# Fused attention, soft mixture of experts and feed-forward: the opening's loads issued together, q on a second queue, and ScalarE's opening order written out

## The chip, the cores and the metric

The kernel runs on one core of one Trainium2 chip. Its time is the device time of one execution in microseconds (us). The engines are named as in the profile: PE (TensorE; PEld is its weight load), DVE (VectorE), ACT (ScalarE), POOL (GpSimd), and SP (SyncE), whose queue issues transfers.

## What is computed

Three layers in one launch, all in float32, with B, H, S, D = 8, 8, 576, 64:

```python
# 1: attention, block causal (blocks of 64 positions)
scores = q @ k.T / sqrt(D); masked where block(query) < block(key)
x = softmax(scores) @ v            # x: 4608 tokens by 512
# 2: soft mixture of experts, 8 experts of 4 slots
logits = x @ phi                   # phi: 512 by 32
slot_input = softmax over tokens(logits).T @ x
slot_out = relu(slot_input[e] @ w1[e]) @ w2[e]
x = softmax over slots(logits) @ slot_out
# 3: feed-forward
h = relu(x @ w_in);  out = (h * h) @ w_out
```

## The kernel before

Attention is worked in 32 pairs of heads, n = 0 to 31: pair n is heads j and j+4 of batch b, with b, j = divmod(n, 4). For a pair, `load_pair(n)` (line 292) issues four transfers of 128 KB, two halves of k and two of q (L298); for the first pair of a batch four more of 64 KB (L305) bring the last 64 positions of k and q of the whole batch. Even batches land in the tile `ar_lo`, odd ones in `ar_hi`; v goes to `ar_hi`. All of these are issued on SP's queue, in SP's order of instructions.

What then happens to a pair, with the names that the profile shows:

- `scale` (line 318): ACT squares k and q and sums them (`square`, L324, tile `junk`); PE adds the sums over partitions (`chain`, L331, `ps_ssq`); eight small DVE operations (L334 to L353) make from them two scales, `sig`, for k and q.
- `split` (line 364): ACT rounds k and q times the scale to float16 (`high`, L383, tiles `ka` and `qa`), DVE makes the rest (`low`, L387); a transfer turns k (`prep_k`, L394, `s<-ka`), and PE turns q (`turn_q`, L403, `ps_qT`), from where ACT copies it out (L407, tile `t`).
- `maxpass` (line 411): PE makes scores for the row maxima (L419, L427, L454, `ps_max`), DVE reduces them (L433), puts the result in extra columns of the low part of q, and a transfer turns this (L480, `t<-qb`). `s2copy` (L895, `s<-s`) copies the turned low part of k beside constants.
- `scores` (L496, L505, L514, `ps_sc`) with the exponentials on ACT (L534, L516), then `pv` (L569 to L606) with v.

The function `pair(n)` (line 925) interleaves these for neighbouring pairs: `scores(n)`, `maxpass(n + 2)`, `split(n + 3)`, `pv(n - 1)`. Loads wait in a list, `dq`; `loads(k)` issues up to k from its front. In the opening (lines 888 to 920) pairs 0 to 2 are prepared ahead of the loop. PE's order inside the loop is the order of the code (`manual_schedule`); the order of the other engines, and of SP's transfers, is chosen by the tile scheduler from the dependences and the order of the code.

```python
loads(12)
prepare()
order = lambda p: [p[2], p[0], p[3], p[1]]   # prep_k, high_q, low_q, turn_q
...
loads(LR if n else 1)                        # in pair(n), eight times; LR = 4
```

The scheduler gives each transfer one of eight semaphores in turn; a transfer waits until the one eight before it has landed.

Of the kernel before, what the change touches and what calls it, by code (L numbers as in the profile page):

```python
# [23 lines left out]
def tile_attn_soft_moe_ffn(  # L24
# [12 lines left out]
    nc = tc.nc  # L37
# [168 lines left out]
    def attention():  # L206
# [82 lines left out]
                in_=phi.rearrange("(hp j p) s -> hp p j s", hp=2, p=64)[hp],  # L289
            )  # L290

        def load_pair(n):
            b, j = divmod(n, NJ)
            t = qk_tile(b)

            def main(nm, hp):
                src = dict(q=q, k=k)[nm][b]
                nc.sync.dma_start(  # L298
                    out=t[nm][:, hp:2 * NU:2, j, :],
                    in_=src[NJ * hp + j, 0:128 * NU, :].rearrange("(u p) d -> p u d", p=128),  # L300
                )

            def tail(nm, hp):
                src = dict(q=q, k=k)[nm][b]
                nc.sync.dma_start(  # L305
                    out=t[nm][64 * hp:64 * hp + 64, 2 * NU],
                    in_=src[NJ * hp:NJ * hp + NJ, 128 * NU:S, :].rearrange("j i d -> i j d"),
                )

            fs = []  # L310
            for nm in "kq":
                for f in (tail, main) if j == 0 else (main,):
                    fs += [lambda f=f, nm=nm, hp=hp: f(nm, hp) for hp in range(2)]
            return fs
# [3 lines left out]
        def scale(ns):  # L318
            w = len(ns)
            small = lambda nm, k=2, bufs=2: sm_p.tile([128, k, 2], F32, tag=nm, name=nm, bufs=bufs)[:, :, 0:w]  # L320
            ssq = sm_p.tile([128, 2, w], F32, tag=f"ssq{w}", name="ssq")

            def square(i, nm, c):
                nc.scalar.activation(  # L324
                    out=junk, in_=qk_tile(ns[c] // NJ)[nm][:, :, ns[c] % NJ, :], func=AF.Square, accum_out=ssq[:, i, c:c + 1],
                    saturate=False,
                )

            def chain():
                ps = ps_r.tile([128, 512], F32, tag="r", name="ps_ssq")  # L330
                nc.tensor.matmul(ps[:, 0:2 * w], ones[:, 0:1].to_broadcast([128, 128]), ssq.rearrange("p a c -> p (a c)"), start=True, stop=True)  # L331
                a, hb, g, inv = [small(nm) for nm in ("sc_a", "sc_h", "sc_g", "inv")]
                sig, es = small("sig", bufs=4), small("es", 1, 4)
                nc.vector.tensor_scalar(  # L334
                    out=a, in0=ps[:, 0:2 * w].rearrange("p (a c) -> p a c", a=2), scalar1=1e-30, scalar2=None, op0=ALU.max
                )
                nc.vector.tensor_scalar(
                    out=hb.bitcast(U32), in0=a.bitcast(U32), scalar1=1, scalar2=0x7F800000,
                    op0=ALU.logical_shift_right, op1=ALU.bitwise_and,
                )  # L340
                nc.vector.tensor_scalar(
                    out=g.bitcast(U32), in0=hb.bitcast(U32), scalar1=0x7F800000, scalar2=None,
                    op0=ALU.bitwise_xor,
                )
                nc.vector.tensor_scalar(out=sig, in0=g, scalar1=2.0 ** -51, scalar2=None, op0=ALU.mult)
                nc.vector.tensor_scalar(out=inv, in0=hb, scalar1=2.0 ** 50, scalar2=None, op0=ALU.mult)
                nc.vector.scalar_tensor_tensor(
                    out=sig[:, 1], in0=inv[:, 0], scalar=2.0 ** 20, in1=sig[:, 1], op0=ALU.mult, op1=ALU.min
                )
                nc.vector.scalar_tensor_tensor(  # L350
                    out=inv[:, 1], in0=sig[:, 0], scalar=2.0 ** -20, in1=inv[:, 1], op0=ALU.mult, op1=ALU.max
                )
                nc.vector.scalar_tensor_tensor(  # L353
                    out=es[:, 0], in0=inv[:, 0], scalar=1.0 / float(D) ** 0.5, in1=inv[:, 1],
                    op0=ALU.mult, op1=ALU.mult,
                )
                for c, n in enumerate(ns):
                    sc[n] = (sig[:, :, c], es[:, 0, c:c + 1])

            return [lambda i=i, nm=nm, c=c: square(i, nm, c) for c in range(w) for i, nm in ((1, "k"), (0, "q"))] + [chain]  # L360
# [3 lines left out]
        def split(n):  # L364
            b, j = divmod(n, NJ)
            if n in (1, 3):
                qa, ka = [
                    xT_p.tile([128, S], F32, tag="xt", name=nm).bitcast(F16).rearrange("p (s a d) -> p s a d", a=2, d=D)
                    for nm in ("qa", "ka")
                ]  # L370
                qa = qa[:, :, 0, :]
            else:
                qa = nat_p.tile([128, NBLK, D], F16, tag="qa", name="qa")
                ka = nat_p.tile([128, NBLK, 2, D], F16, tag="ka", name="ka")
            tr = (tr_a, tr_a, even, odd)[j]
            t1 = tr.tile([128, NBLK, 128], F16, tag="t1", name="t1")
            s1 = tr.tile([128, NBLK, 128], F16, tag="s1", name="s1")
            qbn, s2n = qb[n % NBQ], s2[n % NB2]
            T[n] = [t1, s1, None, s2n]
            r = qk_tile(b)  # L380

            def high(nm, i, hi):
                nc.scalar.activation(out=hi, in_=r[nm][:, :, j, :], func=AF.Copy, scale=sc[n][0][:, i:i + 1])  # L383

            def low(nm, i, hi, lo):
                x = r[nm][:, :, j, :]
                nc.vector.scalar_tensor_tensor(  # L387
                    out=lo, in0=x, scalar=sc[n][0][:, i:i + 1], in1=hi, op0=ALU.mult, op1=ALU.subtract
                )

            def prep_k():
                high("k", 1, ka[:, :, 0, :])
                low("k", 1, ka[:, :, 0, :], ka[:, :, 1, :])
                nc.sync.dma_start_transpose(out=s1, in_=ka.rearrange("p s a d -> p (s a d)"))  # L394

            high_q = lambda: high("q", 0, qa)
            low_q = lambda: low("q", 0, qa, qbn[:, :, 0:D])

            def turn_q(s0, s1_):
                ps = ps_r.tile([128, 512], F32, tag="r", name="ps_qT").bitcast(F16)  # L400
                for s in range(s0, s1_):
                    for h in range(2):
                        nc.tensor.transpose(  # L403
                            ps[64 * h:64 * h + 64, 128 * (s - s0):128 * (s - s0) + 128], qa[:, s, :], id16,
                            tile_position=(0, 64 * h),
                        )
                nc.scalar.copy(t1[:, s0:s1_, :].rearrange("p s c -> p (s c)"), ps[:, 0:128 * (s1_ - s0)])  # L407

            return [high_q, lambda: [turn_q(0, 8), turn_q(8, NBLK)], prep_k, low_q]
# [476 lines left out]
            return decode(dec_p, tin[:, a, 512 * c:512 * c + 512], raws.pop(i), 512)  # L886

        AHEAD, LOOK, LR = 3, 7, 4
        dq = load_pair(0) + load_pair(1) + load_pair(2) + load_pair(3)

        def loads(k):
            for _ in range(min(k, len(dq))):
                dq.pop(0)()

        s2copy = lambda n: nc.sync.dma_start(out=s2[n % NB2][0:64], in_=T[n][1][0:64])  # L895
        loads(12)
        prepare()
        order = lambda p: [p[2], p[0], p[3], p[1]]
        for f in scale([0]) + order(split(0)):
            f()  # L900
        loads(4)
        for f in scale([1]) + order(split(1)) + scale([2]):
            f()
        sp2 = split(2)
        sp2[2]()
        loads(4)
        s2copy(0)
        m0 = maxpass(0)
        for f in m0[6:] + m0[:6] + [sp2[0], sp2[1], sp2[3]]:
            f()  # L910
        dq += load_v(0) + load_pair(4) + load_pair(5) + load_v(1) + [lambda hp=hp: load_phi(hp) for hp in range(2)]
        s3 = scale([AHEAD])
        m1 = maxpass(1)
        for i, f in enumerate(m1[6:] + m1[:6]):
# [10 lines left out]
        def pair(n):  # L925
# [78 lines left out]
            for i in range(8):  # L1004
                for f in slot.get(i, []):
                    f()
                if i == 2 and n + 1 < N:
                    dq.insert(0, lambda: s2copy(n + 1))
                loads(LR if n else 1)
                if aux:  # L1010
                    aux.pop(0)()
                elif decq and i % 8:
                    decq.pop(0)()
                for _ in range((i in (1, 3, 4, 6, 7)) if n < N - 3 else 1 if n < N - 1 else 2):
                    if work:
                        work.pop(0)()
# [386 lines left out]
```

## Time and profile before

| | |
|---|---|
| three runs, median (lowest to highest) | 965.77 us (964.23 to 967.51) |
| the profiled execution's own time | 967.0 us |
| its span | 965.2 us |
| PE, PEld, DVE, ACT, POOL busy, share of the span | 91%, 67%, 62%, 53%, 26% |
| granted TensorE clock, mean | 0.969 |
| HBM read, written | 78.71 MB, 9.44 MB |
| chain of waits: PE, DVE, DMA, ACT | 64%, 11%, 9%, 5% |

Attention takes about the first 465 us, the experts the next 55, the feed-forward the rest. In a timeline a row is one instruction or a run of equal ones: start in us, duration in us, engine, line, operation and tiles, how many, and in brackets how long the engine sat idle before and what ended that. `SPq` is SP's queue; its durations are the issue of a transfer, not the transfer. In the table of stretches a row has, after the stretch, the busy us of PE, PEld, DVE, ACT and POOL with the number of instructions, the granted clock of TensorE (1.00 is 2.4 GHz, 0.50 is 1.2 GHz), the mean busy share of the 16 DMA engines, and GB/s.

### The profile page before, as it was taken

The page shows a single profiled execution, that of the slowest core. Times are in us where ns is not written, and L with a number is a line of the kernel's source. Part 1 is how long each engine was busy: PE and PEld are TensorE (multiplying, and loading weights), DVE is VectorE, ACT ScalarE, POOL GpSimd, SP SyncE. Part 2 cuts the span into 40 slices and gives each one's busy share as a digit, 9 for nine tenths or more (in the row PEclk, how much of TensorE's full clock was granted, in tenths as well). Part 3 has the DMA queues.
Part 4 walks back from the last instruction along what each step waited for, and adds up shares of the span by engine and source line. Part 5 has one row for each costly group of instructions (what it writes and reads, how often), then busy time and mean ns, then how long its engine had stood idle before and what let it go on. Part 6 is the DMA issues. An engine that isn't in the chain of part 4 may idle for free.

```text
span 965.2 us, 19357 instructions
## 1 busy us (share of the span) xinstructions
PE 878.1 (91%) x7614; PEld 650.1 (67%) x7614; DVE 596.4 (62%) x1355; ACT 514.5 (53%) x914; POOL 249.0 (26%) x390
## 2 busy tenths in 40 slices
PE   3758988988998998999998999999999999999997
PEld 2435766666565666666534777888888888888885
DVE  7746797978798796853723886444444445344442
ACT  6558777766767766644224866334434334334432
POOL 0323746545473646564000322000000000000000
PEclk9778999999899999999997999999999999999999
DMA  6767897998899877597997040100001001001002
GB/s 148 148 144 150 168 194 166 168 190 173 158 175 139 169 122 170 105 256 194 343 359 269 5 169 12 55 1 35 31 1 56 11 1 66 1 0 66 1 1 66
DMA packets 225180, 113.01 MB, mean 117 GB/s; under 512 B 193856, under 2 KB 202048, under 8 KB 225088
## 3 DMA queue, kind: packets, MB, share of 16 engines
q1 hardware_dynamic: 225088, 111.77, 49.8%
q8 instruction: 59, 0.97, 0.4%
q14 instruction: 33, 0.27, 0.1%
HBM read 78.71 MB, written 9.44 MB: 91 GB/s over the span
## 4 chain that ended last, share of the span: by engine, by line
PE 64%; DVE 11%; DMA 9%; ACT 5%; POOL 4%; SPq 3%; issue 3%; DVEq 0%; ACTq 0%
PE po L1336 12%; PE po L1338 12%; PE po L1337 12%; PE xm L569 5%; PE ps_sc L496 4%; PE ps_h L1282 3%; DMA raw<-in_moe_w_in_dram 3%; DVE pm L433 2%; POOL ss L539 2%; PE ps_max L419 2%; PE ps_h L1119 1%; POOL ul L679 1%; PE tl L580 1%; PE ps_x L774 1%; DMA s<-s 1%
## 5 line engine op out<-in xcount | busy, mean ns | idle before, releaser
L1337 PE MATMUL po<-wol,gh 128*128 128x512 f32 x576 | 224.3, 389 | 1.2 <-POOL wol L1266 1.2
L1336 PE MATMUL po<-woh,gh 128*128 128x512 f32 x576 | 223.2, 389 | 1.0 <-ACT woh L1265 1.0
L1338 PE MATMUL po<-woh,gl 128*128 128x512 f32 x576 | 223.9, 389 | 0.0
L1292 ACT ACTIVATE r<-ps_h 128x768 f32<-128x768 f32 (+1 forms) x97 | 78.1, 806 | 204.3 <-PE ps_h L1282 204.3
L1299 DVE TENSOR_TENSOR sq<-r 128x768 f32<-128x768 f32 x80 | 76.7, 958 | 170.5 <-ACT r L1292 170.5
L534 ACT ACTIVATE p<-ps_sc,es 128x512 f32<-128x512 f32 x192 | 129.3, 694 | 47.2 <-PE ps_sc L505 28.7
L539 POOL TENSOR_TENSOR ss<-p 128x384 f32<-128x384 f32 (+1 forms) x128 | 85.4, 688 | 206.4 <-ACT p L534 206.1
L433 DVE TENSOR_REDUCE pm<-ps_max 128x4 f32<-128x512 f32 x160 | 107.6, 683 | 49.4 <-PE ps_max L427 48.5
L1336 PEld LDWEIGHTS po<-woh,gh 128*128 128x128 f32 x576 | 108.1, 188 | 24.3 <-ACT woh L1265 1.3
L1338 PEld LDWEIGHTS po<-woh,gl 128*128 128x128 f32 x576 | 108.1, 188 | 22.5
L1337 PEld LDWEIGHTS po<-wol,gh 128*128 128x128 f32 x576 | 108.1, 188 | 20.8 <-POOL wol L1266 1.7
L496 PE MATMUL ps_sc<-t,s 128*128 128x512 f16 (+3 forms) x512 | 109.1, 308 | 7.2 <-DMA s<-s 4.1
L1300 DVE TENSOR_TENSOR gl<-sq,gh 128x768 fp32r<-128x768 f32 (+1 forms) x97 | 93.1, 960 | 17.5 <-ACT sq L1297 7.5
L539 POOL TENSOR_TENSOR ss<-ss,p 128x320 f32<-128x320 f32 (+1 forms) x128 | 98.5, 770 | 17.1 <-ACT p L534 6.0
L569 PE MATMUL xm<-p,ar_hi 128*64 128x256 f32 (+3 forms) x512 | 93.5, 464 | 0.0
L1293 ACT ACTIVATE gh<-r 128x768 fp32r<-128x768 f32 (+1 forms) x97 | 81.6, 841 | 2.8
L419 PE MATMUL ps_max<-s,t 128*128 128x128 f16 (+3 forms) x256 | 63.4, 313 | 13.2 <-ACT t L407 7.1
L580 PEld LDWEIGHTS tl<-p,ar_hi 128*64 128x64 f32 x512 | 37.9, 144 | 38.2 <-issue 33.8
L505 PEld LDWEIGHTS <-s 128*128 128x128 f16 x512 | 46.2, 101 | 15.9 <-issue 3.4
L505 PE MATMUL ps_sc<-t,s 128*128 128x64 f16 x512 | 54.7, 196 | 0.7 <-DVE pm L433 0.4
L1282 PE MATMUL ps_h<-cts,ws 128*128 128x512 f32 x192 | 50.3, 344 | 2.7 <-ACT r L1292 2.4
L496 PEld LDWEIGHTS <-s 128*128 128x128 f16 x512 | 37.3, 102 | 11.5 <-DMA s<-s 4.8
(212 smaller groups left out, 1337.1 us busy)
## 6 DMA issues: line engine op xcount, KB each, us to landing
wch<-in_moe_w_dram SPq DMA_DIRECT2D x12, 1024.0 KB, 8.6
ar_hi<-in_v_dram SPq DMA_DIRECT2D x64, 128.0 KB, 2.8
raw<-in_moe_w_in_dram SPq DMA_DIRECT2D x16, 512.0 KB, 5.2
wch<-in_moe_w_dram SPq DMA_DIRECT2D x16, 512.0 KB, 9.6
out_dram<-ot SPq DMA_DIRECT2D x32, 256.0 KB, 2.1
ar_hi<-in_moe_w_dram SPq DMA_DIRECT2D x6, 1024.0 KB, 7.7
s<-s SPq DMA_DIRECT2D x32, 144.0 KB, 2.9
ar_lo<-in_k_dram SPq DMA_DIRECT2D x32, 128.0 KB, 3.2
```

Of the source, the lines that this page charges most:

```text
L419: nc.tensor.matmul(ps[:, c0:c0 + 128 * (u + 1)].rearrange("p (s c) -> p s c", c=128), t1[:, 2 * u + hp, :], s1[:, hp:2 * u + 2:2, :], star ...
L433: nc.vector.tensor_reduce(out=o, in_=i, axis=AX.X, op=ALU.max)
L496: nc.tensor.matmul(ps[:, c0:c0 + w].rearrange("p (s c) -> p s c", c=128), kk[:, 2 * t + hp, :], qq[:, 2 * u0 + hp:8:2, :], start=(c0 == 0 ...
L505: nc.tensor.matmul(ps[:, c0:c0 + 64], kk[:, 2 * t + hp, :], qq[:, 8, h0:h0 + 64], start=(c0 == 0 and not second), stop=(second and last),)
L534: nc.scalar.activation(out=pt, in_=ps, func=AF.Exp, scale=es[:, 0:1])
L539: add = lambda o, x, y: nc.gpsimd.tensor_tensor(out=o, in0=x, in1=y, op=ALU.add)
L569: nc.tensor.matmul(box["xm"][64 * hp:64 * hp + 64, 128 * t:512], vs[:, t, hp, :], r, start=(t == 0), stop=(t == 3),)
L1293: nc.scalar.activation(out=gh[:, p], in_=r[:, p], func=AF.Square)
L1300: nc.vector.tensor_tensor(out=gl[:, p], in0=sq[:, p], in1=gh[:, p], op=ALU.subtract)
L1336: nc.tensor.matmul(pos[t], gh[:, sl], woh[f], start=(f == 0), stop=False)
L1337: nc.tensor.matmul(pos[t], gh[:, sl], wol[f], start=False, stop=False)
L1338: nc.tensor.matmul(pos[t], gl[:, sl], woh[f], start=False, stop=(f == KF - 1))
```

## The change

Four things are edited. All 20 loads of pairs 0 to 3 are issued first, and those of q of pairs 0 and 1 by ACT's queue. ACT's order in the opening is that of the code, in which ka comes before qa, the squares of pair 1 come before pair 0's q is turned, and those of pair 2 before pair 1's. In the list of loads, v of pair 1 goes ahead of pair 5's k and q. And in the loop's first pass up to four loads per step are issued instead of one, so that the later loads of this list, phi among them, come at other places among SP's transpositions.

```diff
@@ -289,20 +289,20 @@
                 in_=phi.rearrange("(hp j p) s -> hp p j s", hp=2, p=64)[hp],
             )
 
-        def load_pair(n):
+        def load_pair(n, by={}):
             b, j = divmod(n, NJ)
             t = qk_tile(b)
 
             def main(nm, hp):
                 src = dict(q=q, k=k)[nm][b]
-                nc.sync.dma_start(
+                by.get(nm, nc.sync).dma_start(
                     out=t[nm][:, hp:2 * NU:2, j, :],
                     in_=src[NJ * hp + j, 0:128 * NU, :].rearrange("(u p) d -> p u d", p=128),
                 )
 
             def tail(nm, hp):
                 src = dict(q=q, k=k)[nm][b]
-                nc.sync.dma_start(
+                by.get(nm, nc.sync).dma_start(
                     out=t[nm][64 * hp:64 * hp + 64, 2 * NU],
                     in_=src[NJ * hp:NJ * hp + NJ, 128 * NU:S, :].rearrange("j i d -> i j d"),
                 )
@@ -886,29 +886,32 @@
             return decode(dec_p, tin[:, a, 512 * c:512 * c + 512], raws.pop(i), 512)
 
         AHEAD, LOOK, LR = 3, 7, 4
-        dq = load_pair(0) + load_pair(1) + load_pair(2) + load_pair(3)
+        dq = load_pair(0, dict(q=nc.scalar)) + load_pair(1, dict(q=nc.scalar)) + load_pair(2) + load_pair(3)
 
         def loads(k):
             for _ in range(min(k, len(dq))):
                 dq.pop(0)()
 
         s2copy = lambda n: nc.sync.dma_start(out=s2[n % NB2][0:64], in_=T[n][1][0:64])
-        loads(12)
+        loads(len(dq))
         prepare()
-        order = lambda p: [p[2], p[0], p[3], p[1]]
-        for f in scale([0]) + order(split(0)):
-            f()
-        loads(4)
-        for f in scale([1]) + order(split(1)) + scale([2]):
-            f()
-        sp2 = split(2)
-        sp2[2]()
-        loads(4)
-        s2copy(0)
-        m0 = maxpass(0)
-        for f in m0[6:] + m0[:6] + [sp2[0], sp2[1], sp2[3]]:
-            f()
-        dq += load_v(0) + load_pair(4) + load_pair(5) + load_v(1) + [lambda hp=hp: load_phi(hp) for hp in range(2)]
+        with tc.manual_schedule(engines={mybir.EngineType.Activation}):
+            c0, c1, c2 = [scale([i]) for i in range(3)]
+            for f in c0[:2] + c1[:1] + c0[2:]:
+                f()
+            sp0 = split(0)
+            for f in (sp0[2], sp0[0], c1[1], c1[2], sp0[1], sp0[3]):
+                f()
+            sp1 = split(1)
+            for f in (sp1[2], sp1[0], c2[0], c2[1], sp1[1], sp1[3], c2[2]):
+                f()
+            sp2 = split(2)
+            sp2[2]()
+            s2copy(0)
+            m0 = maxpass(0)
+            for f in m0[6:] + m0[:6] + [sp2[0], sp2[1], sp2[3]]:
+                f()
+        dq += load_v(0) + load_pair(4) + load_v(1) + load_pair(5) + [lambda hp=hp: load_phi(hp) for hp in range(2)]
         s3 = scale([AHEAD])
         m1 = maxpass(1)
         for i, f in enumerate(m1[6:] + m1[:6]):
@@ -1006,7 +1009,7 @@
                     f()
                 if i == 2 and n + 1 < N:
                     dq.insert(0, lambda: s2copy(n + 1))
-                loads(LR if n else 1)
+                loads(LR)
                 if aux:
                     aux.pop(0)()
                 elif decq and i % 8:
```

How this moves instructions, at three places.

ACT at the start of the program (`junk` is the square, with `ar_lo` as source the tile of pairs 0 to 3). Before:

```order
L324 ACT_TABLE_LOAD
L324 ACTIVATE junk_151,ssq_219<-ar_lo_72 128x576 x2
L324 ACTIVATE junk_151,ssq_273<-ar_lo_72 128x576
L383 ACTIVATE qa_220<-ar_lo_72,sig_232 128x576
L383 ACTIVATE ka_221<-ar_lo_72,sig_232 128x9x64
L324 ACTIVATE junk_151,ssq_273<-ar_lo_72 128x576
L407 COPY t1_222<-ps_qT_247 128x1024
```

and with the change:

```order
L305 DMA ar_lo_72<-in_q_dram 64x4x64 x2
L298 DMA ar_lo_72<-in_q_dram 128x4x64 x4
L324 ACT_TABLE_LOAD
L324 ACTIVATE junk_151,ssq_229<-ar_lo_72 128x576 x2
L324 ACTIVATE junk_151,ssq_230<-ar_lo_72 128x576
L383 ACTIVATE ka_252<-ar_lo_72,sig_241 128x9x64
L383 ACTIVATE qa_251<-ar_lo_72,sig_241 128x576
L324 ACTIVATE junk_151,ssq_230<-ar_lo_72 128x576
L407 COPY t1_253<-ps_qT_276 128x1024
```

ACT issues six loads ahead of its first square, and rounds k before q. On PE the product `ps_ssq` of pair 1 moves with it: it stood behind the 18 transposes of pair 0's q, and now stands ahead of them, right behind that of pair 0.

SP around the first transposition of a low part of q (`t_391`, now `t_393`: pair 0; `s_345`, now `s_351`: k of pair 2). Before:

```order
L895 DMA s_0_145<-s_223 64x1152
L276 DMA ar_hi<-in_v_dram 128x4x64
L282 DMA ar_hi<-in_v_dram 64x64 x2
L276 DMA ar_hi<-in_v_dram 128x4x64
L394 DMA_TRANSPOSE s_345<-ka 128x9x128
L305 DMA ar_hi<-in_k_dram 64x4x64 x2
L480 DMA_TRANSPOSE t_391<-qb_142 128x9x128
```

and with the change:

```order
L895 DMA s_0_145<-s_254 64x1152
L305 DMA ar_hi<-in_k_dram 64x4x64
L394 DMA_TRANSPOSE s_302<-ka 128x9x128
L298 DMA ar_hi<-in_k_dram 128x4x64 x2
L305 DMA ar_hi<-in_q_dram 64x4x64 x2
L298 DMA ar_hi<-in_q_dram 128x4x64 x2
L394 DMA_TRANSPOSE s_351<-ka 128x9x128
L276 DMA ar_hi<-in_v_dram 128x4x64
L282 DMA ar_hi<-in_v_dram 64x64 x2
L480 DMA_TRANSPOSE t_393<-qb_142 128x9x128
```

Between the copy of pair 0 and this transposition now stand pair 1's transposition and all of pair 4's loads.

SP at the loads of pair 5 (into `ar_hi`) and the transposition of pair 4's k (`s_634`, now `s_652`). Before, the last half of pair 5's q stands behind it:

```order
L895 DMA s_0_145<-s_345 64x1152
L305 DMA ar_lo<-in_q_dram 64x4x64 x2
L298 DMA ar_lo<-in_q_dram 128x4x64
L394 DMA_TRANSPOSE s_634<-ka 128x9x128
L298 DMA ar_lo<-in_q_dram 128x4x64
L298 DMA ar_hi<-in_q_dram 128x4x64
L276 DMA ar_hi<-in_v_dram 128x4x64
```

and with the change both halves stand here, 19 rows of this listing ahead of `s_652`:

```order
L298 DMA ar_hi<-in_k_dram 128x4x64
L895 DMA s_1_146<-s_302 64x1152
L298 DMA ar_hi<-in_k_dram 128x4x64
L298 DMA ar_hi<-in_q_dram 128x4x64 x2
L480 DMA_TRANSPOSE t_483<-qb_143 128x9x128
L287 DMA phi_62<-in_moe_phi_dram 64x4x32
L394 DMA_TRANSPOSE s_492<-ka 128x9x128
```

The second half of q has moved ahead of two transpositions of low parts of q (pairs 1 and 2) and of the k of pairs 3 and 4.

## Rows read from the trace of the kernel before

**Rows 1.** Stretches: span, busy us per engine (instructions), PE clock, transfer share, GB/s.
```profile
0.00:20.00 20.00, 6.25 (x56) 4.76 (x57) 13.16 (x87) 11.90 (x24) 0.70 (x6) 1.00 0.71 150
20.00:40.00 20.00, 14.16 (x123) 8.19 (x122) 15.90 (x48) 11.03 (x22) 3.75 (x6) 0.74 0.72 146
40.00:60.00 20.00, 10.30 (x137) 6.81 (x133) 10.93 (x36) 9.25 (x18) 7.28 (x11) 0.79 0.64 138
60.00:65.00 5.00, 4.49 (x22) 1.73 (x23) 2.66 (x6) 1.91 (x4) 0.00 (x0) 0.50 0.71 152
...
75.00:80.00 5.00, 3.59 (x18) 1.43 (x20) 3.49 (x8) 4.87 (x12) 2.28 (x2) 0.54 0.75 89
80.00:85.00 5.00, 5.00 (x92) 3.48 (x89) 0.00 (x0) 1.16 (x4) 0.00 (x0) 0.78 0.93 208
...
100.00:150.00 50.00, 46.25 (x653) 32.91 (x652) 42.90 (x118) 38.53 (x80) 29.68 (x49) 1.00 0.96 181
```

**Rows 2.** Who waited for whom, whole run: us in total, times, longest us.
```profile
ACT dec_sq L167 <- DMA raw<-in_moe_w_in_dram: 23.8, 11, 3.7
PE ps_ssq L331 <- ACT junk L324: 20.5, 4, 9.7
```

**Rows 3.** Timeline of PE, 0 to 130 us: start, us, instruction, [idle before <- releaser].
```profile
11.64 1.17 PE L403 MATMUL ps_qT<-id,qa 128*64 128x128 f16 x18 [1.67 <-ACT qa L383]
...
57.15 0.58 PE L331 MATMUL ps_ssq<-ssq,ones 128*128 128x2 f32 x2 [9.70 <-ACT junk L324]
...
60.55 0.61 PE L419 MATMUL ps_max<-s,t 128*128 128x128 f16 x2 [0.51 <-ACT t L407]
...
70.38 0.38 PE L331 MATMUL ps_ssq<-ssq,ones 128*128 128x2 f32 x2 [1.24 <-ACT junk L324]
...
76.41 0.61 PE L496 MATMUL ps_sc<-t,s 128*128 128x512 f16 x1 [2.11 <-DMA s<-s]
...
86.92 0.38 PE L419 MATMUL ps_max<-s,t 128*128 128x256 f16 x2 [1.38 <-ACT t L407]
```

**Rows 4.** Timeline of ACT, 0 to 60 us.
```profile
5.80 1.28 ACT L324 ACT_TABLE_LOAD   x1 [5.80 <-DMA ar_lo<-in_k_dram]
...
8.56 0.68 ACT L324 ACTIVATE junk<-ar_lo 128x576 fp8e4<-128x576 f32 x1 [0.70 <-DMA ar_lo<-in_q_dram]
...
10.81 0.77 ACT L383 ACTIVATE qa<-ar_lo,sig 128x576 f16<-128x576 f32 x1 [0.40 <-DVE sig L345]
...
56.32 0.68 ACT L324 ACTIVATE junk<-ar_hi 128x576 fp8e4<-128x576 f32 x1 [5.45 <-DMA ar_hi<-in_q_dram]
```

**Rows 5.** Timeline of SP's queue of transfers, 0 to 75 us: start, issue us, transfer.
```profile
4.72 1.16 SPq L298 DMA_DIRECT2D ar_lo<-in_q_dram  x2
...
13.20 1.43 SPq L394 DMA_TRANSPOSE s<-ka  x1
...
25.09 1.56 SPq L480 DMA_TRANSPOSE t<-qb  x1
...
40.37 1.30 SPq L480 DMA_TRANSPOSE t<-qb  x1
...
51.32 1.33 SPq L394 DMA_TRANSPOSE s<-ka  x1
...
53.32 0.52 SPq L298 DMA_DIRECT2D ar_hi<-in_q_dram  x1
...
73.89 0.51 SPq L895 DMA_DIRECT2D s<-s  x1
```

**Rows 6.** Timeline of DVE around 50 us.
```profile
48.86 0.23 DVE L347 SCALAR_TENSOR_TENSOR sig<-inv,sig 128x1 f32<-128x1 f32 x1
...
50.48 0.81 DVE L387 SCALAR_TENSOR_TENSOR ka<-ar_hi,sig,ka 128x576 f16<-128x576 f32 x1
```

**Rows 7.** Transfers by kind, median us to landing: 0 to 60, then 100 to 200.
```profile
s<-ka SPq DMA_TRANSPOSE x5, 3.5
...
s<-ka SPq DMA_TRANSPOSE x8, 4.5
```
## The prediction

> **What bounds the kernel now.** I read the stretches of the run first, then the waits, then the timelines of PE, ACT, SP and DVE around the longest one. From 100 us on PE sets the time: 46.25 of 50 us busy in one stretch [rows 1]. Before 100 us it does not: 6.25, 14.16 and 10.30 of 20 us in the first three slices, with no other engine full and the transfer engines at 0.64 to 0.72 [rows 1]. So the opening is a chain of waits, and only there can this change act.
>
> The reader should see one wait above all. Of PE's idle time 20.5 us are for ACT's squares (the sums that fix a pair's scales), and one of these waits is 9.70 us long [rows 2, 3]. It ends at 57.15. On ACT the square behind it, at 56.32, sat 5.45 us for a q load into ar_hi [rows 4]. On SP that load, the second half of pair 5's q, was issued at 53.32, behind the transposition at 51.32, which had to wait for DVE's low part of k at 50.48 [rows 5, 6]. SP issues in order, so a load that nothing held back stood behind a transposition that was not ready. PE then reached ps_max of pair 4 at 60.55. After it come two waits of the same family: 1.24 us for another pair's square at 70.38, and 2.11 us at 76.41 for the copy s<-s, issued at 73.89 behind a row of loads [rows 3, 5]. TensorE's granted clock pays as well: 0.50 in 60 to 65, 0.54 in 75 to 80 and 0.78 in 80 to 85, each after such idle time [rows 1].
>
> **The change part by part.** Every sum is against the profiled execution (967.0 us, span 965.2); the median of the three runs shown is 965.77, so the forecast for it lies 1.2 lower.
>
> *q loads of pairs 0 and 1 on ACT.* Now SP issues pair 0's eight loads one behind the other; the two big q loads start at 4.72 and take 1.16 to issue, and ACT waits for them until 8.56, 0.70 us after its square of k [rows 4, 5]. With ACT issuing q beside SP's k, q's square can follow k's at once: a gain of at most 0.8. But pair 0's loads are 768 KB, and at the 181 GB/s of the dense stretch [rows 1] they need 4.3 us whoever issues them; issued from 2 us on they end at 6.3, k 0.4 to 0.5 later than now, and the gain is 0.4. (The Trainium skill, page "DMA: Bandwidth & Descriptors", section "Issuing engines are not separate DMA queues", says that loads of several issuing engines run on the same 16 DMA engines and that a second issuer saves only issue time; by it the gain is the 0.4, by the wait alone 0.8. No run so far shows two issuers.) ACT's price per issue is in no row. Below, 0.58, half of SP's 1.16 for two loads; above, 1.56, SP's dearest issue, a transposition's [rows 5]. Six at 0.58 end at 4.2, before ACT's first work at 5.80 [rows 4], and cost nothing; six at 1.56 end at 10.1, 4.3 late. A plain load is the nearest row, so I take nothing and keep 4.3 as a bound.
>
> *ACT's order.* PE now takes the ssq products of pairs 0 and 1 ahead of pair 0's q transposes, which today follow qa at once: qa 10.81 to 11.6, transposes at 11.64 [rows 3, 4]. Now ka stands in front of qa (0.77 more), the earlier squares take off 0.4 to 0.8, and after qa come pair 1's square of q (0.8) and its ssq product (0.58 [rows 3]): 13.0 to 13.4, some 1.5 later. ka and its transposition gain what qa loses; the later pairs see about +1.0, and DVE, 15.90 of 20 us busy in the second slice [rows 1], leaves little room to win it back.
>
> *All loads of pairs 0 to 3 first; phi later.* SP's first transposition stands at 13.20 because DVE is ready only then [rows 5]; with ka first it could go at 12.2. But 2.5 MB of loads are issued ahead of it, and the copy s<-s four places behind it waits for its landing (3.5 us [rows 7]). Behind that stand the next transposition, pair 4's loads, pair 2's transposition and part of v, some 9.3 us of issue at 0.6 and 1.4 each; so t<-qb of pair 0 goes out at 25 to 26, where it now goes at 25.09 [rows 5]. With landings of 4.5 instead of 3.5 us, as in the dense stretch [rows 7], twice on this path, it is two more late. Opening loss: +1.0 to +3.0; I take +2.0, halfway, since the transfer engines will stand between the two stretches.
>
> *Pair 5's q ahead of the waiting transpositions.* Its load now precedes t<-qb of pair 1 and the transposition of pair 3, so ACT's 5.45 us go. What is late next is the transposition of pair 4, which ps_max of pair 4 needs. DVE's scale of pair 4 ends at 49.09 [rows 6], with the loss at 51.1; ka on ACT takes 0.77 [rows 4], the low part 0.81 [rows 6], so SP can issue at about 52.8, and it lands 3.5 to 4.5 later [rows 7], 56.8 in the middle. SP is free by then: t<-qb of pair 2, now at 40.37 [rows 5], is at 42.4, and 13 plain transfers stand between, 7.5 us. Against 60.55 that is **-3.7** with the loss taken in (-5.2 to -2.2 with the loss at 1.0 or 3.0 and the landing at 3.5 or 4.5).
>
> *The later waits.* The loads of pairs 5 to 9 move forward on SP too, and 1.24 goes. Between pair 4's transposition at 52.8 and the copy now at 73.89 stand 13 plain transfers and three transpositions, 11.8 us: it goes out near 65 and lands near 68, and PE wants it at 76.41 less 2.11, 3.7 and 1.2, 69.4. So 2.11 goes as well: **-3.4** (bounds -1.2, the square's alone, and -4.7, if the 1.38 at 86.92 [rows 3] goes too).
>
> *The clock.* The slow time from 76.41 on (0.54, then 0.78 [rows 1]) is 5.8 us at the lower of the two levels, worth 2.9. Without the idle time ahead of it it may stay away; ACT, 4.87 of 5 us busy in 75 to 80 [rows 1], then limits, so I take half: **-1.4** (0 to -2.9). The slow stretch after 57 I leave: PE will still idle some 5 us before 57.
>
> *The rest.* From pair 8 on the program is the same; the scheduler places some of ACT's and SP's instructions a few slots off. ACT waits 23.8 us, 11 times, for w_in pieces, 3.7 at the longest [rows 2]; one such wait more or less, passed to PE in part, is the most I give it: 0, bounds -2.5 and +2.5. An early gain is kept, since after 100 us each wait hangs on work of the same few pairs and all of it shifts together.
>
> Sum: -3.7 - 3.4 - 1.4 = -8.5: 958.5 for the profiled execution, **957.3 us** for the median. All favourable ends give -15.3 (950.5), all others -0.9 (964.9).
>
> **Rivals.** (a) *The transfer engines are the opening's limit; slower.* The three slices moved 150, 146 and 138 GB/s [rows 1]. Ahead of pair 4's transposition now stand 8.83 MB (ACT's six loads and SP's first 63 transfers, at the sizes of the tiles). If 146 GB/s is all that these small pieces give, that takes 60.5 us from 2 us on, the transposition lands at 66, PE is 5.5 later than at 60.55, nothing behind is gained, and the time is 971. It decides below 162 GB/s (8.83 MB by 56.5). For it: three equal slices. Against: shares of only 0.64 to 0.72 there, 181 GB/s at 0.96 later, 208 at 0.93 in 80 to 85 [rows 1]. 10 in 100.
> (b) *The wait only moves.* ps_max of pair 4 gets its k at 58.3, and the waits at 70 and 76 come back through ACT, nearly full at 75 to 80: -2.2, 963.6. For it: ACT serves squares, copies and exponentials in order, and two of PE's later waits end on it [rows 3]. Against: the first of them is for a load that now comes earlier. 14 in 100.
> (c) *ACT's issues are dear* (1.56 each): 4.3 of the gain lost, 961.6; faster still, and part of the forecast's range.
> (d) *The clock holds through.* With the long idle time cut in two, the slow stretch after 57 goes too (0.50 in 60 to 65 [rows 1]; 7 us of it, some 3.5) and all of the second: 952 to 953, or lower. 6 in 100.
>
> **How the numbers follow.** The forecast, with (c), has 70 in 100 and spans 950.5 to 964.9. Case (a) and the low part of (d) are left out: 951 to 966. A measurement of this kernel tells 0.3%, 2.9 us. Faster: forecast and (d), 0.76; same: (b), 0.14; slower: (a), 0.10.
>
> **What would show it.** Right: no PE wait above 4 us between 40 and 60; pair 5's q squared before 45; ps_max of pair 4 before 58.5, released by its transposition or ACT's copy; the copy s<-s no releaser of PE before 80; transfer share above 0.8 in 0 to 50; pair 0's q transposes near 13, t<-qb of pair 0 issued at 25 to 28. Wrong: slices still at 150 GB/s with transpositions landing after 5 us or more, or an opening that is earlier while the end is not.

## The result, and the profile after

The changed kernel takes 955.92 us (median of 4 runs, 954.59 to 957.15) where the kernel before, beside it, takes 966.64 (4 runs, 964.23 to 967.85): a ratio of 0.9892, 95% interval 0.9865 to 0.9919. The forecast was 957.3, its range 951 to 966. A second series gave 0.9901 (0.9869 to 0.9933; 6 runs against 27). The kernels below were run on several chips, so only ratios to the kernel before on the same chip are compared. The profiled execution took 957.15 us, span 955.4, mean granted clock 0.973 (before 967.0, 965.2 and 0.969).

Stretches of the changed kernel, columns as in [rows 1]:

```profile
0.00:20.00 20.00, 3.45 (x40) 2.87 (x40) 11.23 (x77) 9.67 (x20) 0.70 (x6) 1.00 0.88 162
20.00:40.00 20.00, 13.44 (x105) 8.12 (x106) 15.21 (x51) 11.71 (x24) 1.35 (x3) 0.76 0.78 154
40.00:60.00 20.00, 15.03 (x179) 9.28 (x178) 14.79 (x44) 16.34 (x35) 10.15 (x14) 0.84 0.76 160
60.00:65.00 5.00, 5.00 (x97) 3.46 (x94) 0.78 (x2) 2.22 (x6) 0.00 (x0) 0.90 1.09 147
...
70.00:75.00 5.00, 4.46 (x26) 1.93 (x28) 4.71 (x9) 2.11 (x4) 2.56 (x4) 0.66 0.73 85
75.00:80.00 5.00, 4.56 (x96) 3.45 (x90) 1.79 (x4) 3.76 (x10) 0.00 (x0) 1.00 0.81 170
```

The first slice is worse than before (PE 3.45 us busy instead of 6.25), the third better (15.03 instead of 10.30), and the clock's second fall is a shorter one (0.66 in 70 to 75, where before it was 0.54 in 75 to 80 and 0.78 behind it). PE's timeline shows the same trade:

```profile
10.61 0.59 PE L331 MATMUL ps_ssq<-ssq,ones 128*128 128x2 f32 x2 [10.61 <-ACT junk L324]
14.40 0.59 PE L331 MATMUL ps_ssq<-ssq,ones 128*128 128x2 f32 x2 [3.20 <-ACT junk L324]
14.91 1.17 PE L403 MATMUL ps_qT<-id,qa 128*64 128x128 f16 x18
...
32.53 0.59 PE L496 MATMUL ps_sc<-t,s 128*128 128x512 f16 x1 [2.87 <-DMA t<-qb]
...
57.84 0.58 PE L419 MATMUL ps_max<-s,t 128*128 128x128 f16 x2 [2.42 <-DMA s<-ka]
...
70.54 0.39 PE L496 MATMUL ps_sc<-t,s 128*128 128x512 f16 x1 [1.31 <-DMA s<-s]
```

Pair 0's q transposes start at 14.91 instead of 11.64 [rows 3]. The product that waits for t<-qb starts at 32.53; in the kernel before it is this row:

```profile
28.65 0.58 PE L496 MATMUL ps_sc<-t,s 128*128 128x512 f16 x1 [1.86 <-DMA t<-qb]
```

Then the wait of 9.70 us is gone, ps_max of pair 4 starts at 57.84 instead of 60.55, and of the later waits for s<-s 1.31 us are left. ACT, SP and DVE of the changed kernel at the places that decide this:

```profile
0.74 1.40 ACTq L305 DMA_DIRECT2D ar_lo<-in_q_dram  x2
2.18 3.15 ACTq L298 DMA_DIRECT2D ar_lo<-in_q_dram  x4
7.68 1.28 ACT L324 ACT_TABLE_LOAD   x1 [7.68 <-DMA ar_lo<-in_q_dram]
...
41.85 0.67 ACT L324 ACTIVATE junk<-ar_hi 128x576 fp8e4<-128x576 f32 x1
```
```profile
2.44 4.33 SPq L298 DMA_DIRECT2D ar_lo<-in_k_dram  x6
...
28.31 2.11 SPq L480 DMA_TRANSPOSE t<-qb  x1
...
54.14 1.44 SPq L394 DMA_TRANSPOSE s<-ka  x1
```
```profile
53.30 0.82 DVE L387 SCALAR_TENSOR_TENSOR ka<-ar_hi,sig,ka 128x576 f16<-128x576 f32 x1
```

ACT's first work waits until 7.68 instead of 5.80 [rows 4]. Pair 5's q is squared at 41.85 (the row with that load; 56.32 before). Pair 4's transposition goes out at 54.14, just as DVE ends the low part of k.

To see where a lead is won and kept, this table gives when PE starts the first `ps_sT` (line 633, the last stage of a pair), less the time of the profiled execution before, so that a minus is a lead; "again" is the changed kernel's second trace, e1 to e10 are the runs below. The rows count from 1: row 1 is the kernel's pair 0, row 32 its pair 31. "Pair 3's lead" and "pair 1's last stage", here and in the texts below, mean these rows; loads, squares, transpositions and ps_max keep the kernel's count from 0.

| pair | before | changed | again | e1 | e3 | e4 | e6 | e9 | e10 |
|---|---|---|---|---|---|---|---|---|---|
| 1 | 45.79 | +3.48 | +3.96 | +2.30 | +1.66 | +3.04 | +1.65 | +2.68 | +0.58 |
| 2 | 71.30 | -4.87 | -2.30 | -1.07 | -3.66 | -1.62 | -5.55 | -0.97 | +0.77 |
| 3 | 88.36 | -8.05 | -5.40 | -4.23 | -3.79 | -4.56 | -10.81 | -7.61 | +0.63 |
| 7 | 134.74 | -5.86 | -3.71 | -3.09 | -2.82 | -2.68 | +3.62 | -5.12 | +1.85 |
| 12 | 200.67 | -5.23 | -1.39 | -2.40 | -0.96 | -0.45 | +2.62 | -4.61 | +6.34 |
| 18 | 281.90 | -4.92 | -2.09 | -1.83 | +0.47 | -0.75 | +1.30 | -4.52 | +6.64 |
| 23 | 350.86 | -11.00 | -8.37 | -8.10 | -2.65 | -7.93 | +1.46 | -8.19 | +1.45 |
| 32 | 462.10 | -10.40 | -10.68 | -10.58 | -5.20 | -10.17 | +4.09 | -10.68 | -1.02 |

Two traces of the same changed kernel differ by 2.65 us at pair 3 and by 3.84 at pair 12: leads that differ by less are not told apart by one trace. The traces also come from several chips, on which the kernel before took 962.8 to 966.6 us in the median, and not all are of a usual execution: that of the kernel before took 967.0 us, e6's is the slowest of its twelve, e9's the fastest, e4's the third fastest. So a column tells where its trace gained or lost; what an edit is worth, the ratios of the runs tell.

### The profile page after: what moved, and what is told of

Read it like the earlier page. It is cut to its first block, busy times and chain, and to the rows that moved or that the text cites. A ratio compares the mean times of both kernels' runs of the same rounds, so it can differ in the third digit from the quotient of the medians.

```text
span 955.4 us, 19343 instructions
## 1 busy us (share of the span) xinstructions
PE 875.7 (92%) x7614; PEld 649.9 (68%) x7614; DVE 593.8 (62%) x1355; ACT 513.7 (54%) x914; POOL 244.7 (26%) x390
## 4 chain that ended last, share of the span: by engine, by line
PE 63%; DVE 12%; DMA 10%; ACT 6%; SPq 4%; issue 3%; POOL 2%; ACTq 0%; DVEq 0%
PE po L1339 12%; PE po L1341 12%; PE po L1340 12%; PE xm L569 4%; PE ps_sc L496 4%; PE ps_h L1285 3%; DMA raw<-in_moe_w_in_dram 2%; DVE pm L433 2%; DMA ar_hi<-in_k_dram 2%; PE ps_max L419 2%; DMA s<-s 2%; PE ps_h L1122 2%; DVE dec_hf L171 1%; DVE dec_sq L183 1%; PE ps_u L670 1%
## 5 line engine op out<-in xcount | busy, mean ns | idle before, releaser
L505 PEld LDWEIGHTS <-s 128*128 128x128 f16 x512 | 45.6, 100 | 15.1 <-issue 2.5
```

The source lines that it names most:

```text
L505: nc.tensor.matmul(ps[:, c0:c0 + 64], kk[:, 2 * t + hp, :], qq[:, 8, h0:h0 + 64], start=(c0 == 0 and not second), stop=(second and last),)
```

## The experiments

**The parts apart.** e1 is the kernel before with one line changed, e2 adds the place of v, e3 is the changed kernel without both, e4 the changed kernel with q on SP.

```diff
 e1, e2:  -loads(LR if n else 1)
          +loads(LR)
 e2:      -load_pair(4) + load_pair(5) + load_v(1)
          +load_pair(4) + load_v(1) + load_pair(5)
 e3:      both of these taken back in the changed kernel
 e4:      -load_pair(0, dict(q=nc.scalar)) + load_pair(1, dict(q=nc.scalar))
          +load_pair(0) + load_pair(1)
```

> The kernel before with one edit: in the loop's first pass up to four loads per step are issued instead of one (the other three edits are left out). Theory T (the gain is pair 5's second q load issued ahead of the transposition of pair 4's k; the edits of the opening cost some 3.5 us): the opening stays as before (first work of pair 1's last stage on PE near 45.8 us), the wait of 9.70 us goes, ps_max of pair 4 starts near 54.5 instead of 60.55, pair 3 leads the kernel before by 10 to 11.5, and the time is 953 to 957, as fast as the changed kernel or up to 2.5 us faster. Rival R1 (the gain is in the opening: earlier loads, the second queue, ACT's order): 963 to 967. Rival R2 (the gain comes from where the scheduler happens to put later work): the lead at pair 3 is as in T but shrinks to less than half by pair 12 and is anywhere from 2 to 12 us at the end.

> The kernel before with both edits behind the opening: four loads per step in the first pass, and v of pair 1 ahead of pair 5's k and q. Theory T: pair 5's q still stands ahead of pair 4's transposition, so the same as with the first edit alone, within 1 us (953 to 957); v of pair 1 being four places earlier is worth nothing. Rival R1: 963 to 967. Rival R3 (the place of v matters, PE's later work waits for it): 1.5 us or more faster or slower than the first edit alone.

> The changed kernel with both edits behind the opening taken back: only the opening is changed (all loads first, q by ACT, ACT's order). Pair 5's second q load stands behind the transpositions of low parts of q of pairs 1 and 2 and of pair 3's k, but ahead of that of pair 4's k. Theory T: the opening is 3.5 us late as in the changed kernel (pair 1's last stage at 49.3); ACT's wait for the load is 0 to 3 us instead of 5.45, ps_max of pair 4 at 58 to 61, pair 3 leads by 3 to 7, and the time is 958 to 963. If the load's place alone decides and it is early enough: as the changed kernel, 955 to 957. Rival R1: 954 to 957 without any lateness of the opening as its cause. Rival R4 (without the four loads per step nothing is won): 968 to 970.

> The changed kernel with the q loads of pairs 0 and 1 on SP's queue again (all loads still first, ACT's order kept). Theory T (the second queue let pair 1's loads share the transfer engines with pair 0's, so pair 0's k landed at 7.68 instead of 5.80): the table load starts at 5.8 to 6.2, the first ssq product at 9.4 to 9.8 instead of 10.61, the q transposes of pair 0 at 13.2 to 13.8 instead of 14.91, and the time is 0.5 to 2 us under the changed kernel, 954 to 955.5. Rival R5 (the second queue is a gain, as issue on SP alone is slower): the first ssq product at 10.6 or later and the time 956.5 to 958.5.

Measured, as ratios to the kernel before (31 runs): e1 0.9923 (0.9893 to 0.9953), e2 0.9930 (0.9900 to 0.9960), e3 0.9987 (0.9961 to 1.0013), e4 0.9943 (0.9916 to 0.9970).

The one line in the loop's first pass brings about three quarters of the gain (by its interval, between half and all), v's place nothing that shows, and the opening by itself nothing that shows. R1 falls. R4's words hold (without the four loads per step nothing that shows is won), only its time, slower than before, does not. T's 958 to 963 for e3, written when the kernel before stood at 966.64, is a ratio of 0.991 to 0.996, and e3 does not reach it. PE in e3:

```profile
52.69 0.59 PE L331 MATMUL ps_ssq<-ssq,ones 128*128 128x2 f32 x2 [3.58 <-ACT junk L324]
56.55 0.58 PE L419 MATMUL ps_max<-s,t 128*128 128x128 f16 x2 [0.97 <-DMA s<-ka]
```

In e3, too, pair 5's q is loaded ahead of pair 4's transposition (issued at 47.83). PE's long wait falls to 3.58 us, and ps_max of pair 4 starts at 56.55, earlier than in any trace of the changed kernel; the execution traced took 960.95, near the median of 961.71. So an early ps_max of pair 4 is not enough for the gain.

T was wrong on e1's trace as well. It has no wait for pair 5's q, yet ps_max of pair 4 started at 61.75 where T said 54.5, and pair 3 led by 4.23 instead of 10 to 11.5. Timelines of DVE, SP and PE in e1, then the same three in e4:

```profile
52.17 0.88 DVE L387 SCALAR_TENSOR_TENSOR ka<-ar_hi,sig,ka 128x576 f16<-128x576 f32 x1
```
```profile
58.20 1.49 SPq L394 DMA_TRANSPOSE s<-ka  x1
```
```profile
58.17 0.61 PE L496 MATMUL ps_sc<-t,s 128*128 128x512 f16 x1 [4.69 <-DMA s<-s]
61.75 0.59 PE L419 MATMUL ps_max<-s,t 128*128 128x128 f16 x2 [2.97 <-DMA s<-ka]
```
```profile
52.30 0.88 DVE L387 SCALAR_TENSOR_TENSOR ka<-ar_hi,sig,ka 128x576 f16<-128x576 f32 x1
```
```profile
57.47 1.51 SPq L394 DMA_TRANSPOSE s<-ka  x1
```
```profile
9.62 0.59 PE L331 MATMUL ps_ssq<-ssq,ones 128*128 128x2 f32 x2 [9.62 <-ACT junk L324]
13.40 0.59 PE L331 MATMUL ps_ssq<-ssq,ones 128*128 128x2 f32 x2 [3.19 <-ACT junk L324]
```

In e1 the low part of k is done at 53.05, but its transposition goes out 5.2 us later: in between SP issues, almost without a gap, pair 8's loads and the copy s<-s, and before them those of pairs 6 and 7. In e4 it is 4.3 us late, in the two traces of the changed kernel 0.0 and 1.1. So there the transposition waits for SP's queue. That would be the opening's worth beside the four loads: loads issued in the first 20 us, and six of them by ACT, no longer stand in SP's queue at 50. The runs don't show it by themselves, since the intervals of e1 and of the changed kernel overlap. e4 shows the other side too: with one queue the first ssq product is at 9.62 instead of 10.61, so the second queue, which brings pair 1's loads in beside pair 0's, cost pair 0 1.0 us. e4 starts earlier and over its runs is later (0.9943 against 0.9892 and 0.9901), but these intervals overlap too, and its trace is of one of its fastest executions and ends before both of the changed kernel.

**Two attempts at a better version**, with the changed kernel again beside them as control (e8). e5 gives ACT another opening order; e6 is e1 with fewer loads in the second pass, e7 both edits in the changed kernel.

```diff
 e5, e7:  -for f in c0[:2] + c1[:1] + c0[2:]:
          +for f in c0[:2] + c1[:2] + c0[2:]:
          -(sp0[2], sp0[0], c1[1], c1[2], sp0[1], sp0[3])
          +(sp0[2], sp0[0], c1[2], sp1[2], sp0[1], sp0[3])
 e6:      -loads(LR if n else 1)
 e7:      -loads(LR)
 e6, e7:  +loads(LR if n != 1 else 1)
```

> The changed kernel with another order for ACT's opening: the square of pair 1's q is taken before pair 0's k is rounded (ACT waits 0.87 us for the scale there anyway), and pair 1's k is rounded before pair 0's turned q is copied out. Theory T2 (the order written for ACT costs most of the opening's 3.5 us, since pair 1's ka waits behind the copy of pair 0's q, 17.08 instead of 14.60): the second ssq product at 11.5 to 12.2 instead of 14.40, pair 0's q transposes at 13.5 to 14.2, pair 1's at 16 to 17.2, t<-qb of pair 0 issued at 26 to 27.5, pair 1's last stage at 47 to 48 (49.27 in the changed kernel), pair 3's lead over the kernel before 8.5 to 10, and the time up to 2 us under the changed kernel's. Rival (the loss is contention of the loads, not the order): pair 1's last stage at 48.8 or later, the time within 1 us of the changed kernel's.

> The kernel before with four loads per step in the loop's first pass and one in the second, so that the loads of pairs 7 and 8 don't all stand ahead of the transposition of pair 4's k. Theory T3 (with four loads per step alone SP's queue was the limit: pair 4's low part of k was ready at 52.9, its transposition went out at 58.20 behind loads issued without a gap; in the changed kernel ready at 54.1 and out at 54.14): the transposition goes out at 52.9 to 54, ps_max of pair 4 starts at 56.3 to 57.5 (61.75 with four loads per step in both passes), pair 3 leads the kernel before by 6.5 to 8.5 (4.2 there), as in the changed kernel without any change of the opening, and the time is 953 to 957 against 962.8 for before. Rival (what held pair 4's k is something else, or the loads put off are missed later): lead at pair 3 of 4 to 5, time as with four loads per step alone or slower.

> The changed kernel with both: the other order for ACT's opening and one load per step in the loop's second pass. T2 and T3 together: pair 4's transposition out at 51 to 52.5, ps_max of pair 4 at 54.5 to 56, pair 3's lead 9.5 to 11.5, and the time 1 to 4 us under the changed kernel's. If one of them alone is the limit there, it shows the smaller of the two gains. Rival (placement later in attention decides the end more than these 2 to 3 us): leads at pair 3 as said, but the end not under the changed kernel's.

> The changed kernel as it is, again, on the chip of the other three: a ratio to the kernel before of 0.987 to 0.992 as in its first runs, and the same places in its trace within 0.3 us up to pair 3 (pair 1's last stage at 49.3, pair 4's ps_max at 57.8). If the ratio comes out above 0.994, the first four runs were a favourable draw, and the comparisons with the single edits move with it.

Measured (27 runs of the kernel before): e5 0.9932 (0.9907 to 0.9957), e6 1.0017 (0.9992 to 1.0043), e7 0.9937 (0.9909 to 0.9964), e8 0.9901 (0.9869 to 0.9933). Neither edit beats the change.

e5: the second ssq product came at 12.31 as hoped for, but pair 0's q transposes at 15.44, later than in the changed kernel. DVE explains it:

```profile
11.32 0.16 DVE L334 TENSOR_SCALAR sc_a<-ps_ssq 128x2 f32<-128x2 f32 x1 [3.83 <-PE ps_ssq L331]
12.94 0.16 DVE L334 TENSOR_SCALAR sc_a<-ps_ssq 128x2 f32<-128x2 f32 x1 [1.45 <-PE ps_ssq L331]
13.13 0.24 DVE L337 TENSOR_SCALAR sc_h<-sc_a 128x2 uint32<-128x2 uint32 x2
```

With both products near each other the scheduler interleaves the two chains of small operations, and pair 0's second step waits for pair 1's first: ka of pair 0 is rounded at 13.94 instead of 12.24. Pair 1's last stage came at 48.81, as the rival has it (48.8 or later), but for this reason and not for contention, so T2 isn't settled by it. e7 led most of all at pair 3 and was still not faster than e5 or the changed kernel, as its rival said; its ps_max of pair 4 came at 57.86, not at 54.5 to 56, so its lead has another source than the one that T3 names. e8's places did not repeat within the 0.3 us of its text: pair 1's last stage came at 49.75, ps_max of pair 4 at 59.72.

e6 shows T3's mechanism at its place: DVE ready at 52.5, transposition at 52.54, and at pair 3 the largest lead but one of all kernels, 10.81 (e7 11.33). And then it loses it. SP, ACT's square, PE and one of the stretches where it goes, in e6:

```profile
52.54 1.32 SPq L394 DMA_TRANSPOSE s<-ka  x1
```
```profile
104.44 0.68 ACT L324 ACTIVATE junk<-ar_hi 128x576 fp8e4<-128x576 f32 x1 [2.32 <-DMA ar_hi<-in_q_dram]
```
```profile
55.92 0.58 PE L419 MATMUL ps_max<-s,t 128*128 128x128 f16 x2 [1.85 <-DMA s<-ka]
...
105.85 1.87 PE L670 MATMUL ps_u<-phi,xt 128*128 128x64 f32 x8 [1.86 <-ACT p L534]
```
```profile
105.00:115.00 10.00, 9.15 (x53) 8.18 (x54) 3.05 (x14) 4.02 (x9) 6.58 (x13) 0.55 0.36 81
```

Between pairs 3 and 7 the lead of 10.81 becomes a lag of 3.62. The first 6.2 us of it go before 93 us: PE waits 1.87 us for ACT's exponentials at 80.83 and 1.61 for a copy s<-s at 83.40, and the clock is 0.71 and 0.61 in 80 to 85 and 85 to 90. The rest goes behind row 5: ACT waits for a q load at 104, its exponentials behind that release PE at 105.85, and after that short idle time the granted clock is 0.55 over 10 us. The load at 104 is pair 12's, issued from 97 on, and not one of those put off; the kernel before waits for it too (1.06 us at 104.16). That the loads put off cost e6 its gain follows from the ratios of e6 and e1, which differ by this line alone; by which waits, the trace does not show. In the changed kernel the same line costs nothing that shows (e7 against e5).

**One load, and a later place.** e9 is the changed kernel with the second half of pair 5's q issued where it was before, and e12 the same again; e10 and e11 move the decoding of w_in in the kernel before and in the changed one.

```diff
 e9, e12: -load_v(0) + load_pair(4) + load_v(1) + load_pair(5) + ...
          +load_v(0) + load_pair(4) + load_v(1) + p5[:3] + ...
          +if n == 1 and i == 3: dq.insert(0, p5[3])
 e10, e11: -elif decq and i % 8:
           +elif decq and i > 2:
```

> The changed kernel with one load put back: the second half of pair 5's q is issued right behind the transposition of pair 4's k, as in the kernel before; all else stays. Theory T: the load goes out near 55.5 instead of 33.5, lands near 59.5, ACT's square of it ends near 60.4, PE waits 4 to 7 us for it and ps_max of pair 4 starts at 62 to 65 (57.8 and 59.7 in the two traces of the changed kernel), so that pair 3's lead over the kernel before falls from 5.4 to 8.1 to between 0 and 3. For the end there are two theories. Kept (what is lost at pair 4 stays lost): 958 to 962 where the changed kernel has 953 to 956. Absorbed (from pair 9 on something else sets PE's pace, as the leads of several kernels that were 4 to 8 at pair 3 were 10.2 to 10.7 at pair 32): 953 to 957, with pair 32's lead at 9 or more.

> The kernel with pair 5's second q load put back behind pair 4's transposition, once more, since its first profiled execution was the fastest of its twelve (955.6, their median 960.6) and kept its lead. Theory T (the load costs the 4 to 6 us by which that kernel's median lies above the changed kernel's): again a median of 958 to 962 and a ratio to the kernel before of 0.994 to 0.999; in a profiled execution near the median PE's wait for the square is again 8 to 10 us, ps_max of pair 4 starts at 61.5 to 63.5, and the time is lost as lower granted clock or as waits before pair 3 or behind it (mean clock 0.967 to 0.972, where the changed kernel has 0.973 to 0.976). Rival (the first median was a draw): 954 to 957.

> The kernel before with one edit far behind the opening: the decoding of w_in, whose first operation is ACT's dec_sq, starts at the fourth step of a pass instead of the second, so that its piece has landed when ACT comes to it. Theory D (the change won part of its time in pairs 15 to 23, where ACT in the kernel before waits for such pieces, 23.8 us in 11 waits against 15 to 18 in 6 or 7): ACT's waits for w_in pieces fall below 16 us, the opening stays (pair 3's lead within 1 us of 0), the lead at pair 23 is 3 to 8, and the time is 956 to 960 against 962.8 for before. Rival (these waits lie off PE's path): within 2 us of the kernel before, whatever ACT's waits do.

> The changed kernel with the same edit of the decoding. If the change already has what theory D gives: within 1.5 us of the changed kernel's 953.2 to 955.9. If the waits left (15.2 to 17.9 us) still cost PE time: 1.5 to 4 us faster, 950 to 953. If a later decode is missed elsewhere (its output is needed only after attention, but its pieces share two buffers): slower by up to 3.

Measured: e9 0.9965 (0.9936 to 0.9994), e12 0.9957 (0.9933 to 0.9981), e10 1.0004 (0.9977 to 1.0031), e11 0.9896 (0.9855 to 0.9937). ACT and PE in e9:

```profile
58.36 0.68 ACT L324 ACTIVATE junk<-ar_hi 128x576 fp8e4<-128x576 f32 x1 [4.80 <-DMA ar_hi<-in_q_dram]
```
```profile
59.19 0.59 PE L331 MATMUL ps_ssq<-ssq,ones 128*128 128x2 f32 x2 [9.06 <-ACT junk L324]
...
62.12 0.61 PE L419 MATMUL ps_max<-s,t 128*128 128x128 f16 x2
```

With that one load late, ACT's wait is back (4.80 us) and so is PE's (9.06 us); over 24 runs the ratio is 0.006 to 0.007 above the changed kernel's, some 6 us of its 10 (an estimate; the intervals leave about 3.5 to 9). So in the changed kernel the place of this load is worth more than half of the gain, in the time that T's "kept" gave. T's way to it is not borne out: pair 3's lead was to fall to between 0 and 3 and is 7.61. The traces don't show where those 6 us are lost: ps_max of pair 4 starts 2.1 to 4.3 us later (62.12 and 61.80) than in the two traces of the changed kernel, but at pair 3 and at pair 32 the lead is as theirs. Each of the two profiled executions (955.62 and 954.96) was the fastest of its twelve, at clocks of 0.976 and 0.977; the means over all twelve were 0.9706 and 0.9726, against 0.9735 and 0.9760 for the changed kernel. Pooled, that is 0.9716 against 0.9750, and 0.0034 of some 930 us is, as an estimate, 3 of the 6 us; where the usual execution loses the rest, no trace of one shows. Together with e3, where this wait was short and nothing was gained, it stays open by which way the place of this load comes to count in the end.

Theory D is not borne out: in e10 ACT's waits for w_in pieces fell from 23.8 to 18.7 us, where below 16 was meant, and nothing was gained. In e11 they stayed as they were (15.1 us), so it tests nothing more; it equals the changed kernel. No run is reliably faster than the change.

## Why the prediction was right, point by point

**What bounds the kernel: right for the traces, not shown for the runs.** Worked out from the 20 stretches of 5 us each before 100 us: PE's idle time there fell from 35.8 to 31.6 us, and busy time times (1 - granted clock), the part lost to the clock, from 10.2 to 6.8; together 7.6 us of the span's 9.8. But in e3 the same sum falls by 4.3 us (to 33.6 and 8.1), and e3 is not faster than the kernel before.

**q on ACT: price right, effect wrong.** ACT's six issues took 0.37 to 0.73 us each and ended at 5.33, with 1.0 us of waiting among them, before its first work: rival (c) falls. The gain of 0.4 to 0.8 did not come. The term counted pair 0's 768 KB alone; pair 1's q now came in on the second queue beside them, and the median landing of k in 0 to 60 rose from 2.9 to 4.2 us. e4 prices that at 1.0 us. By the Trainium skill, page "DMA: Bandwidth & Descriptors", section "Issuing engines are not separate DMA queues", a second issuer saves only issue time, usually small beside the transfer. The runs agree on the sharing; "small" misleads here, since just that issue time, six loads off SP's queue, lets pair 4's transposition go out earlier (54.14 and 55.66 against 57.47).

**The opening's loss: too small.** Forecast +2.0 (+1 to +3), measured +3.9 at the wait for t<-qb and +3.5 at pair 1. Pair 0's q transposes were forecast for 13.0 to 13.4 and came at 14.91, 1.5 to 1.9 late. The landing explains all of it: the squares were to be 0.4 to 0.8 earlier, and the first ssq product came 1.2 later; what ACT's order adds there was reckoned rightly. Further on the order does cost: it puts ka of pair 1 behind the copy of pair 0's q, here in the kernel before and in the changed one, 2.5 us later, of which the landing is 1.2.

```profile
14.60 0.77 ACT L383 ACTIVATE ka<-ar_lo,sig 128x576 f16<-128x576 f32 x1
```
```profile
17.08 0.79 ACT L383 ACTIVATE ka<-ar_lo,sig 128x576 f16<-128x576 f32 x1
```

t<-qb went out at 28.31, just past the upper end of 25 to 28, and in the second trace at 30.23.

**Pair 5's q: right in mechanism up to ps_max, the size within its bounds in one trace of two.** ps_max of pair 4 was forecast at 56.8, with its bounds (-5.2 to -2.2) 55.4 to 58.3, and came at 57.84, released by its transposition. In the second trace it came at 59.72, 0.8 us ahead of the kernel before instead of 3.7, where the transposition stood 1.1 us behind its input:

```profile
55.66 1.47 SPq L394 DMA_TRANSPOSE s<-ka  x1
```
```profile
59.72 0.58 PE L419 MATMUL ps_max<-s,t 128*128 128x128 f16 x2 [2.65 <-DMA s<-ka]
```

"SP is free by then" was true by 0.2 us in one trace and failed by 1.1 in the other; e1 and e4 show the queue as the limit. The prediction counted the 13 plain transfers rightly, but gave them 7.5 us from 43.7 on; they took 8.3 from 45.56 on. And that an early ps_max is time at the end, e3 does not bear out (56.55, and nothing gained).

**The later waits and the clock: right as a sum.** -4.8 forecast, -5.3 measured (pair 3's lead of 8.05 less the 2.71 at ps_max). The 1.24 went; the 2.11 became 1.31. The clock's part was -1.2 against -1.4: 75 to 85 is at 1.00 now, worth 2.7 us by the rows of before, and 70 to 75 at 0.66 costs 1.5 (0.34 of 4.46 busy). The sign that the copy s<-s would release no wait of PE before 80 failed: it did at 54.81 (0.57 us) and at 70.54 (1.31).

**The rest: wrong in its reason.** That an early gain is kept because "all of it shifts together" does not hold. The changed kernel's lead is 8.05 at pair 3, 3.70 at pair 15 and 11.00 at pair 23; e6's 10.81 became a loss. The change brought some 2 to 6 us more between pair 3 and the end (spans 9.8 and 11.2 shorter, leads at pair 3 of 8.05 and 5.40), which the term of 0 did not have, and by luck that covered the opening's excess. In their traces the kernels with four loads per step in the first passes end attention 8.7 to 11.1 us ahead of the one trace before, whatever they led by at pair 3, e3 without them 5.2. What makes up the difference in pairs 15 to 23 was tried once (e10) and not found.

**The rivals.** (a) fell in its time: pair 4's transposition let PE go at 57.84 and not at 66, and the shares rose to 0.88, 0.78 and 0.76, so the transfer engines had had room. The rate was near its line all the same: 159 GB/s over the first 60 us, against the 162 below which it was to decide. (The 8.83 MB are right; SP's transfers in them are 65, not 63.) (b) came true in a small part (2.42 and 1.31 us of new waits). (d) half, and in one trace: the clock was at 0.90 in 60 to 65, but low until 60, and in the second trace 0.57 in 60 to 65.

## What to carry to other kernels

Read an in-order issue queue as an engine with its own busy time: ask at each urgent transfer when its input was ready and when it went out, and if work lies between, move plain loads to idle time or to another queue. Move them earlier rather than later: in e6 the loads put off won 11 us at pair 3 and lost 14 by pair 7, though in e7 the same edit cost nothing that shows. And an early lead, or a long wait that is gone, is not yet time at the end: follow it with a few marks through the run, take two traces before a difference of 3 us is believed, and let the runs decide.

## What was not expected of the hardware

A row of several issues holds the waits between them too. With two engines issuing at the start, the row at 2.44 spans 4.33 us for six loads, which looks like 0.72 us each. Its fourth issue alone, and who SP's queue waited for in the first 10 us (us in total, times, longest):

```profile
5.24 0.37 SPq L298 DMA_DIRECT2D ar_lo<-in_k_dram  x1
```
```profile
SPq L298 <- DMA ar_lo<-in_k_dram: 1.0, 1, 1.0
SPq L298 <- DMA ar_lo<-in_q_dram: 0.2, 1, 0.2
```

The six issues take 0.37 to 0.64 us each, as in e4 with SP alone (0.51 to 0.62); the rest is SP standing until earlier loads have landed, which they do later here. So the second queue did not make issues dearer, it made SP wait.

Two executions of one program differed by 0.35 us in the landing that ACT's first work waits for (7.68 and 8.03) and by 2.65 us at pair 3, in part by the granted clock, which fell at 70 to 75 in one (0.66) and at 80 to 85 in the other (0.66).
